# Moving the score stores of two batches from SyncE's DMA queue to ScalarE's, in a one-core talking-heads attention and expert kernel

## The chip, the cores and the metric

The kernel runs on one core of one Trainium2 chip. The metric is the device time of one execution in microseconds (us). Before the change three runs gave 1441.49 to 1446.57 us, with a median of 1444.0 us. The profile is of one further execution.

The engines are named as the profile names them: PE (TensorE; PEld is its weight load), DVE (VectorE), ACT (ScalarE), POOL (GpSimd) and SP (SyncE). SP computes nothing here: it issues DMAs. Before the change it issues every one of them.

## What is computed

```python
scores = np.matmul(q, k.transpose(0, 1, 3, 2)) / np.sqrt(64)   # q, k, v: 8 batches, 12 heads, 448, 64
scores = np.einsum('bhij,hg->bgij', scores, w_pre)             # mix the 12 heads
attn = np.exp(scores - np.max(scores, axis=-1, keepdims=True))
attn = attn / (np.sum(attn, axis=-1, keepdims=True) + 1e-09)
attn = np.einsum('bhij,hg->bgij', attn, w_post)                # mix them again
x = np.matmul(attn, v)                                         # heads side by side: 3584 x 768
h = (x @ w1) * (x @ w2) @ w3                                   # 768 -> 1024, 1024 -> 1024
out = h @ w_out                                                # 1024 -> 768
```

The weights w1, w2, w3 and w_out arrive as 64-bit numbers and are turned into 32-bit ones on the chip.

## The kernel before

**Scores.** `qk` (line 166) computes one score tile: two heads of a batch, the pair `p` (0 to 5), for 128 query rows, the tile `c`. Tiles 0, 1 and 2 are rows 0 to 383; `c == 3` joins the last 64 rows of two pairs. PE writes the two heads into two PSUM banks (`psq`), ACT copies them into an SBUF tile `st` (lines 179 and 180), and a DMA stores `st` in `raw_d[b]`, a DRAM array of all heads of a batch. `qk` doesn't issue this DMA: it returns a function, `store`, that does. The `st` tiles come from pools with two buffers: odd pairs of batch 0 have a pool of their own (`qp`), all others share `kp`. So the copy into a buffer waits until the store from it has landed.

**Rows read back.** The mixing works on 20 query rows of all 12 heads at a time, called a set. `fetch(m)` (line 195) reads the rows of set `m` from `raw_d` into `r`, of which there are two. `mix(m)` (line 214) multiplies them by w_pre into PSUM, `largest` and `exp` make the softmax, `scale` and `post` the second mixing, and `put` (line 272) copies the result into `mt`. `av` multiplies by v once 150 rows are there.

**Steps.** The loop at line 889 runs over steps `n`, two to a set. A step first does what is at its start: in an even step `fetch(m + 2)`, then `do_later()` (line 83), which calls the functions put aside, the stores of the step before among them, then loads of v and of the next q and k. Then come the pieces of weight conversion, softmax or second mixing, and background matmuls. Last come the `qk` of the step, whose `store` goes into `later` (line 982). So on SP a score store stands behind the fetch of the next step. Steps 0 to 11 have one `qk` of batch 0 each, steps 12 to 14 one for its last rows; batch 1 adds its own from step 11 on, about three in four steps.

**The first tile.** For `c == 0` of batch 0 all pairs go into one wide tile `sz`. Before the loop the upper 48 rows (`FIRST`) are stored pair by pair, and the other 80 rows of all heads by one DMA of 1680 KB, made at line 805 and issued where `held()` is called (line 881), after the fetches of sets 0 and 1 and one load of weight words.

**Weight words.** In the first steps `converting` (line 132) turns words into 32-bit weights: a load `cs`, up to five ahead, a square on ACT (`cm`, line 110), four operations on DVE (`cx`, lines 121 to 124) and a split into two parts by ACT (line 129) and POOL (line 130).

**DMA semaphores.** In the built program each DMA, on whichever queue, adds to one of eight semaphores, DMAHW0 to DMAHW7, mostly in turn, and first waits until the DMA before it on the same semaphore has landed. So a DMA waits, as a rule, for the one issued eight before it in the order of the program.

Of the kernel before, what the change touches and what calls it, by code (L numbers as in the profile page):

```python
# [21 lines left out]
QT, NJ = 128, 4  # L22
# [5 lines left out]
PP = 64  # L28
JB = S // PP
SETS = NB * B // 2  # L30
FIRST = 48
# [19 lines left out]
class Kernel:  # L51
# [114 lines left out]
    def qk(self, b, p, c, banks):  # L166


        nc = self.nc
        ps = [self.bank(i, f"psq{b}_{p}_{c}_{s}")[:, :S] for s, i in enumerate(banks)]  # L170
        for z, (t, q, k) in enumerate(self.parts(b, p, c)):
            for s in range(2):
                rows = slice(s * D, (s + 1) * D)
                nc.tensor.matmul(ps[s][z * PP:(z + 1) * PP], t[rows, q:q + PP], t[rows, k:k + S], start=True, stop=True)  # L174
        if b == c == 0:
            st = self.sz[:, 2 * p:2 * p + 2]
        else:
            st = (self.qp if b == 0 and p % 2 else self.kp).tile([128, 2, S], F32, tag="st", name=f"st{b}_{p}_{c}", bufs=2)
        nc.scalar.copy(st[:, 0], ps[0])  # L179
        (nc.vector.tensor_copy if b == c == 0 else nc.scalar.copy)(st[:, 1], ps[1])  # L180
        raw = self.raw_d[b]
        if c == 3:
            def store():
                for z in range(2):
                    nc.sync.dma_start(raw[3 * QT:, 2 * (p + z) - 2:2 * (p + z)], st[z * PP:(z + 1) * PP])
            return store
        n = QT if b or c else FIRST
        return lambda: nc.sync.dma_start(raw[c * QT:c * QT + n, 2 * p:2 * p + 2], st[:n])

# [549 lines left out]
    def run(self):  # L741
        nc, tc = self.nc, self.tc
# [52 lines left out]
        held = []  # L795
# [6 lines left out]
        next(fold_pieces)  # L802
        for f in held:
            f()
        held = lambda: nc.sync.dma_start(self.raw_d[0][FIRST:QT], self.sz[FIRST:])

# [3 lines left out]
        for b in range(1, B):  # L812
            first, per = (11, 28 / 21) if b == 1 else ((b - 1) * NB - 6, NB / 21)
            units = [(b, p, c) for g in range(0, HP, 2) for p, c in [*itertools.product((g, g + 1), range(3)), (g + 1, 3)]]
            for i, (b, p, c) in enumerate(units):
                n = int(first + i * per) | (b > 1)
# [3 lines left out]
        for b in range(B):  # L820
            for a in range(NG):
                for g in range(HP):
                    n = (b * NB + (a + 1) * GB + 3) | 1
# [54 lines left out]
            self.fetch(m)  # L878
        next(fold_pieces)
        next(fold_pieces)  # L880
        held()
        next(fold_pieces)
        next(fold_pieces)
        self.mix(0)
# [4 lines left out]
        for n in range(N + 6):  # L889
# [45 lines left out]
            p, pieces = self.n_made - 1 if fold_pieces else 2 * KF + 3 * KF, None  # L935
            if avs.get(n):
                pass
            elif fold_pieces:
                f = (self.n_made - 1 - 2 * KF) // 3
# [39 lines left out]
                self.mix(m + 1)  # L979
            self.do_ends()  # L980
            for i, x in enumerate(qks.get(n, [])):
                self.later.append(self.qk(*x, (6, 7) if i else (0, 1)))
            if third:
                next(unit_pieces)

# [66 lines left out]
```

## Time and profile before

| | |
|---|---|
| median of three runs | 1444.0 us |
| the three runs | 1446.57, 1441.49, 1444.0 us |
| profiled execution, its own time | 1437.83 us |
| its span, first to last instruction | 1436.1 us |
| PE busy | 1382.4 us, 96% |
| ACT busy | 832.4 us, 58% |
| DVE busy | 741.1 us, 52% |
| POOL busy | 620.3 us, 43% |
| granted PE clock, mean | 0.986 |

Times in the rows of the profile count from the start of the span. A timeline row gives start, duration, engine, line, operation, the tiles out and in, and in brackets how long the engine sat idle before it and what the profile takes to have ended that. "DMA share" in a table of windows is the mean busy share of the 16 DMA engines, "GB/s" what they moved, "(x...)" a number of instructions. "us to landing" counts from the issue of a DMA.

### The profile page before, as it was taken

Reading aid. Unit: us, or ns where it says so; the run is one execution under the profiler, and the core shown is the slowest. Engines: PE = TensorE matmul, PEld = TensorE weight load, DVE = VectorE, ACT = ScalarE, POOL = GpSimd, SP = SyncE. Lnnn points to the kernel's source line nnn. Section 1 sums busy time; section 2 is a strip of 40 time slices with the busy share of each in tenths; the row PEclk is TensorE's granted clock in tenths of the full one; section 3 lists DMA queues with packets and bytes.
Section 4 is the critical chain, followed back from the end, with each engine's and each line's share of the span. In section 5 each row is a group of like instructions: output and inputs, shape, how many; then the busy total and the mean of one; then the engine's idle time right before and its main releaser. Section 6 shows DMA issues by size and latency. Waiting matters only on the chain.

```text
span 1436.1 us, 45775 instructions
## 1 busy us (share of the span) xinstructions
PE 1382.4 (96%) x18684; PEld 1055.2 (73%) x18684; DVE 741.1 (52%) x1497; ACT 832.4 (58%) x1952; POOL 620.3 (43%) x754
## 2 busy tenths in 40 slices
PE   5889999999999999999999999999999999999998
PEld 2457786776677667776777777777777777899988
DVE  6867566767544544432444436334444446345563
ACT  4867666777766666665656556556555445422231
POOL 2433233434433544532345336334335446446693
PEclk7989999999999999999999999999999999999999
DMA  8998789999999999999989979799879757698775
GB/s 294 366 326 279 236 270 322 320 312 317 324 286 348 355 356 330 362 346 349 287 275 290 320 259 280 249 323 354 288 229 281 241 177 223 195 337 270 231 232 171
DMA packets 203761, 416.87 MB, mean 290 GB/s; under 512 B 20528, under 2 KB 120112, under 8 KB 203472
## 3 DMA queue, kind: packets, MB, share of 16 engines
q1 hardware_dynamic: 203552, 413.94, 87.6%
q8 instruction: 149, 2.44, 0.7%
q14 instruction: 60, 0.49, 0.1%
HBM read 279.77 MB, written 134.09 MB: 288 GB/s over the span
## 4 chain that ended last, share of the span: by engine, by line
PE 82%; DMA 8%; DVE 4%; ACT 2%; issue 1%; POOL 1%; SPq 0%; DVEq 0%; POOLq 0%; ACTq 0%
PE e L702 21%; PE psa L301 11%; PE pso L260 10%; PE psm L220 9%; PE psq L174 7%; PE eg L522 5%; PE psf L360 4%; PE eo L553 4%; PE e2o L702 4%; PE e1o L702 4%; PE e3o L702 4%; DMA wu<-w_d 3%; DMA r<-raw_d 2%; DMA raw_d<-st 2%; ACT e L235 1%
## 5 line engine op out<-in xcount | busy, mean ns | idle before, releaser
L247 POOL TENSOR_SCALAR w<-wpo,ri 128x60 f32<-128x60 f32 x360 | 180.7, 518 | 485.1 <-DVE ri L245 465.3
L227 DVE TENSOR_REDUCE mn<-psm 128x1 f32<-128x448 f32 x360 | 207.7, 618 | 321.6 <-PE psm L220 321.3
L274 ACT COPY mt<-pso 128x480 f32<-128x480 f32 x352 | 197.9, 621 | 185.8 <-PE pso L260 185.6
L702 PE MATMUL e<-eh,wu 128*128 128x448 f32 x1008 | 296.8, 371 | 6.4 <-DVE c L656 3.2
L235 ACT ACTIVATE e<-psm,mn 128x448 f32<-128x448 f32 x360 | 226.8, 643 | 7.9 <-DVE mn L227 7.9
L702 PEld LDWEIGHTS e<-eh,wu 128*128 128x128 f32 x1008 | 187.5, 188 | 52.2 <-issue 26.8
L260 PEld LDWEIGHTS pso<-w,e 60*64 60x64 f32 x10080 | 175.2, 135 | 51.0 <-issue 42.5
L220 PE MATMUL psm<-r,wsc 60*64 60x448 f32 (+1 forms) x1440 | 191.2, 550 | 19.1 <-DVE cx L124 8.3
L260 PE MATMUL pso<-w,e 60*64 60x60 f32 x10080 | 199.1, 224 | 0.4 <-ACT mt L274 0.3
L702 PE MATMUL e<-el,wu 128*128 128x448 f32 x504 | 186.9, 371 | 0.0
L301 PE MATMUL psa<-mt,v 128*64 128x150 f32 (+1 forms) x2304 | 156.9, 292 | 4.1 <-ACT st L179 4.1
L301 PEld LDWEIGHTS psa<-mt,v 128*64 128x64 f32 x2304 | 143.6, 137 | 20.1 <-ACT st L179 6.7
L174 PE MATMUL psq<-kq 64*64 64x448 f32 x1176 | 154.6, 542 | 2.4 <-ACT st L179 2.4
L656 DVE TENSOR_TENSOR c<-c,e 128x448 f32<-128x448 f32 x168 | 101.7, 618 | 87.7 <-PE e L702 82.9
L179 ACT COPY st<-psq 128x448 f32<-128x448 f32 x162 | 86.4, 533 | 73.7 <-ACT mt L274 34.1
L522 PE MATMUL eg<-xh,wu 128*128 128x448 f32 x384 | 119.2, 381 | 6.3 <-DMA wu<-w_d 6.3
L641 POOL TENSOR_TENSOR el<-x,eh 128x448 fp32r<-128x448 f32 x90 | 103.7, 1170 | 32.8 <-ACT eh L640 29.9
L702 PEld LDWEIGHTS e<-el,wu 128*128 128x128 f32 x504 | 94.6, 188 | 22.5 <-issue 14.1
L174 PEld LDWEIGHTS psq<-kq 64*64 64x64 f32 x1176 | 60.8, 135 | 56.4 <-issue 28.8
L522 PEld LDWEIGHTS eg<-xh,wu 128*128 128x128 f32 x384 | 71.9, 190 | 38.7 <-issue 24.0
L244 DVE TENSOR_SCALAR sa<-sm 128x2 f32<-128x2 f32 x180 | 34.9, 194 | 113.6 <-ACT e L235 113.1
L180 ACT COPY st<-psq 128x448 f32<-128x448 f32 x162 | 87.6, 541 | 0.0
(99 smaller groups left out, 2010.1 us busy)
## 6 DMA issues: line engine op xcount, KB each, us to landing
r<-raw_d SPq DMA_DIRECT2D x344, 210.0 KB, 5.1
raw_d<-st SPq DMA_DIRECT2D x138, 448.0 KB, 6.1
wu<-w_d SPq DMA_DIRECT2D x104, 384.0 KB, 6.7
wu<-s_d SPq DMA_DIRECT2D x96, 384.0 KB, 4.8
wu<-w_d SPq DMA_DIRECT2D x51, 512.0 KB, 5.5
kq<-kq SPq DMA_DIRECT2D x42, 448.0 KB, 7.0
wu<-s_d SPq DMA_DIRECT2D x36, 512.0 KB, 4.9
x<-x_d SPq DMA_DIRECT2D x72, 224.0 KB, 5.7
```

The costliest lines, as they stand in the source:

```text
L174: nc.tensor.matmul(ps[s][z * PP:(z + 1) * PP], t[rows, q:q + PP], t[rows, k:k + S], start=True, stop=True)
L220: nc.tensor.matmul(ps[s][c * PP:(c + 1) * PP, :S], self.wsc[k], r[k, c], start=True, stop=True)
L227: self.nc.vector.tensor_reduce(mn[:, s:s + 1], self.psm[m][s][:, :S], axis=AX.X, op=ALU.min)
L235: nc.scalar.activation(e, p[:, :S], AF.Exp, bias=mn[:, s:s + 1], scale=-1.0, accum_out=sm[:, s:s + 1])
L247: nc.gpsimd.tensor_scalar_mul(w2[:, s], self.wpo, ri[:, s:s + 1])
L260: nc.tensor.matmul(self.pso[c][z * PP:(z + 1) * PP, at:at + HK], e[k, j * PP:(j + 1) * PP], w2s[k, s], start=True, stop=True)
L274: self.nc.scalar.copy(dst.rearrange("p j g (s i) -> p j s g i", s=2), src)
L301: nc.tensor.matmul(self.psa[rows, g % 3, :W], v[:, j, rows], mt[:, j, 2 * g + s, :W], start=(j == 0), stop=(j == NJ - 1))
L522: nc.tensor.matmul(p, u[:, k % (K1 // 2), x], xs[y][:, k], start=(k == 0 and t == 0), stop=(k == K1 - 1 and t == 2))
L641: nc.gpsimd.tensor_tensor(lo, x, hi.bitcast(F32), op=ALU.subtract)
L656: nc.vector.tensor_tensor(a[out], a[to[0]], p, op=ALU.add)
L702: nc.tensor.matmul(p, w[:, k, x], ops[m, k][y], start=(k == 0 and t == 0), stop=(k == nk - 1 and t == 2))
```

## The change

Three edits move 44 DMA issues to ACT. First, the score stores of batches 0 and 1 are issued on ACT's DMA queue (`nc.scalar`), all but the upper 48 rows of the first tile. Second, in the loop these stores are called right behind the copies of their `qk`, and not put into `later`; those of batches 2 to 7 stay as they were. Third, the 80 lower rows of the first tile go out in two DMAs, of 16 and of 64 rows, also on ACT.

```diff
-        raw = self.raw_d[b]
-        if c == 3:
-            def store():
+        raw, dma = self.raw_d[b], nc.sync.dma_start if b > 1 or b == c == 0 else nc.scalar.dma_start
+
+        def store():
+            if c == 3:
                 for z in range(2):
-                    nc.sync.dma_start(raw[3 * QT:, 2 * (p + z) - 2:2 * (p + z)], st[z * PP:(z + 1) * PP])
-            return store
-        n = QT if b or c else FIRST
-        return lambda: nc.sync.dma_start(raw[c * QT:c * QT + n, 2 * p:2 * p + 2], st[:n])
+                    dma(raw[3 * QT:, 2 * (p + z) - 2:2 * (p + z)], st[z * PP:(z + 1) * PP])
+            else:
+                n = QT if b or c else FIRST
+                dma(raw[c * QT:c * QT + n, 2 * p:2 * p + 2], st[:n])
+
+        return store
...
-        held = lambda: nc.sync.dma_start(self.raw_d[0][FIRST:QT], self.sz[FIRST:])
+        held = [lambda k=k: nc.scalar.dma_start(self.raw_d[0][k], self.sz[k]) for k in (slice(FIRST, PP), slice(PP, QT))]
...
-        held()
+        for f in held:
+            f()
...
-                self.later.append(self.qk(*x, (6, 7) if i else (0, 1)))
+                store = self.qk(*x, (6, 7) if i else (0, 1))
+                if x[0] > 1:
+                    self.later.append(store)
+                else:
+                    store()
```

The new lines shift the code: line 188 of before is 189 of after, 202 is 205, 805 is 808.

The first place is SP's queue before the loop, before the change. `cs3` to `cs5` are loads of weight words, `r1` is the second set's rows, and L805 stores the 80 rows.

```order
L202 DMA r1_222<-raw0_d_62 60x2x448 [waits DMAHW6_49]
L103 DMA cs3_225<-wo 128x768
L805 DMA raw0_d_62<-sz_136 80x5376
L103 DMA cs4_238<-wo 128x768 [waits DMAHW1_49]
L103 DMA cs5_240<-wo 128x768 [waits DMAHW2_49,DVE_49,Activation_49]
```

After the change the 80 rows stand on ACT, as two DMAs between a square (`cm1`) and a split (`fw0`) of the weight conversion:

```order
L129 CAST fw0_227<-cx0_210 128x3x128 [waits DVE_49]
L110 ACTIVATE cm1_230<-cs1_151 128x384 [waits DMAHW1_49,Activation_49]
L808 DMA raw0_d_62<-sz_136 16x5376 [waits DMAHW5_49]
L808 DMA raw0_d_62<-sz_136 64x5376 [waits DMAHW7_49]
L129 CAST fw0_227<-cx1_232 128x3x128 [waits DVE_49]
L110 ACTIVATE cm2_245<-cs2_206 128x256 [waits DMAHW6_49,Activation_49]
```

On SP `cs4` now follows `cs3` directly.

The second place is SP at steps 10 to 13, before the change. In a name such as `st1_0_1` stand batch, pair and tile; `w34` is a stored piece of folded weights.

```order
L188 DMA raw0_d_62<-st0_4_2_784 128x896 [waits DMAHW1_49,Activation_49]
L286 DMA v0_5_789<-v 128x512 [waits DMAHW2_49]
L103 DMA cs18_791<-wo 128x768 [waits DMAHW3_49,DVE_49]
L202 DMA r8_863<-raw0_d_62 60x2x448 [waits DMAHW4_49,PE_49]
L202 DMA r8_863<-raw0_d_62 60x2x448 [waits DMAHW5_49]
L188 DMA raw0_d_62<-st0_5_2_851 128x896 [waits DMAHW6_49,Activation_49]
L188 DMA raw1_d_63<-st1_0_0_860 128x896 [waits DMAHW7_49,Activation_49]
```

After the change ACT has these stores, each behind its own two copies; here steps 10 and 11 on ACT:

```order
L179 COPY st0_4_2_785<-psq0_4_2_0_779 128x448 [waits PE_49]
L180 COPY st0_4_2_785<-psq0_4_2_1_780 128x448 [waits PE_49]
L189 DMA raw0_d_62<-st0_4_2_785 128x896 [waits DMAHW4_49,Activation_49]
L129 CAST fo_148<-cx13_769 128x384 [waits DVE_49]
L110 ACTIVATE cm14_803<-cs14_577 128x384
L277 COPY mt0_0_415<-pso0_141 128x4x2x12x5 [waits PE_49]
L277 COPY mt0_0_415<-pso1_142 128x4x2x12x5 [waits PE_49]
L179 COPY st0_5_2_852<-psq0_5_2_0_846 128x448 [waits DMAHW1_49,PE_49]
L180 COPY st0_5_2_852<-psq0_5_2_1_847 128x448 [waits PE_49]
L189 DMA raw0_d_62<-st0_5_2_852 128x896 [waits DMAHW0_49,Activation_49]
```

The store of `st0_5_2` no longer stands behind the fetch of `r8`; what ACT does next now stands behind the store and the semaphores that it waits for.

## The prediction

> **What bounds the kernel now.** I read the windows first, then the chain of waits of the first 110 us, then the timelines of ACT, SP and DVE around its longest pieces. The windows (engine busy times, granted clock, DMA share, GB/s):
>
> ```profile
> core 0: us, PE busy (x) PEld busy (x) DVE busy (x) ACT busy (x) POOL busy (x), PEclk, DMA share, GB/s
> 14.00:16.00 2.00, 0.00 (x0) 0.00 (x0) 1.86 (x4) 0.30 (x1) 0.58 (x1) 0.50 0.60 179
> 18.00:20.00 2.00, 1.84 (x9) 0.93 (x13) 0.09 (x1) 0.41 (x1) 0.72 (x1) 0.50 0.85 197
> 28.00:62.00 34.00, 29.02 (x424) 15.16 (x425) 31.95 (x63) 29.39 (x71) 14.25 (x19) 0.86 1.02 354
> 62.00:96.00 34.00, 25.42 (x294) 13.38 (x286) 23.54 (x44) 21.67 (x52) 11.53 (x14) 0.80 1.03 367
> 96.00:112.00 16.00, 15.06 (x263) 11.60 (x263) 7.27 (x15) 10.27 (x25) 3.77 (x6) 1.00 0.66 212
> 120.00:150.00 30.00, 30.00 (x403) 22.84 (x402) 24.17 (x48) 22.48 (x56) 10.84 (x15) 1.00 0.96 308
> 150.00:200.00 50.00, 49.36 (x686) 39.33 (x685) 30.66 (x64) 33.01 (x80) 14.44 (x21) 1.00 0.80 255
> ```
>
> Four stages follow. Until 28 us the DMA engines are not full and others wait. From 28 to 62 DVE is full (31.95 of 34), ACT nearly (29.39), and the DMA share is 1.02. From 62 to 96 PE, DVE and ACT all have idle time and only the DMA engines are full. From 96 PE is (15.06 of 16, 30.00 of 30). The stores moved are those of the first three stages and of the fourth up to about 190 us; what is won before 96 us should stay won, since PE then works through a fixed order.
>
> The chain of waits of that stretch (start, us, what):
>
> ```profile
> 17.18 0.42 SPq L805
> 17.65 10.36 DMA cs<-wo
> ...
> 60.76 8.07 DMA r<-raw_d
> 68.96 1.50 PE psm L220 x8
> 71.09 7.26 DMA raw_d<-st
> ...
> 87.56 8.09 DMA raw_d<-st
> 95.72 0.54 ACT st L179
> ```
>
> Its long pieces are transfers: a load of words issued behind the 80-row store, a fetch, and two score stores.
>
> **The change part by part.**
>
> *A, the first tile.* On DVE:
>
> ```profile
> 25.33 0.17 DVE L245 RECIPROCAL ri<-sa 128x2 f32<-128x2 f32 x1
> 28.10 0.36 DVE L121 TENSOR_SCALAR cx<-cs 128x384 int32<-128x384 int32 x1 [2.60 <-DMA cs<-wo]
> ```
>
> DVE waits 2.60 us for the load issued at 17.65. The 1680 KB ahead of it take 4.7 us at the 367 GB/s of 62 to 96. On ACT they stand behind the second square and so start some 2 to 3 us earlier, while the engines move only 179 and 197 GB/s, and the load no longer queues behind them. At best the 2.60 go. At worst half of the 4.7 us comes ahead of the fetches of the first sets and delays all by 2.3. Nearer the first, as the engines had room: **-1.5** (-2.6 to +2.3). The share below 1 between 14 and 20 us is also what limits it: no more than about 2 us of transfer time lay idle.
>
> *B, steps 0 to 10 (28 to 62 us).* The pace is that of DVE, and ACT waits twice in two steps:
>
> ```profile
> 36.93 1.14 DVE L227 TENSOR_REDUCE mn<-psm 128x1 f32<-128x448 f32 x2
> 43.69 1.14 DVE L227 TENSOR_REDUCE mn<-psm 128x1 f32<-128x448 f32 x2
> ...
> 40.73 0.51 ACT L129 CAST fo<-cx 128x384 fp32r<-128x384 f32 x1 [0.64 <-DVE cx L124]
> 43.80 0.51 ACT L129 CAST fo<-cx 128x384 fp32r<-128x384 f32 x1 [0.20 <-DVE cx L124]
> ```
>
> Two steps take 43.69 - 36.93 = 6.76 us; ACT's idle time in them is 0.64 + 0.20 = 0.84. The trace shows no DMA issued on ACT; the nearest rows are SP's issues of the same stores, with their times to landing (minimum, median, maximum):
>
> ```profile
> L188 SPq DMA_DIRECT2D raw_d<-st x23: 325/349/1124, 28.8 to 128.3; - x23
> L185 SPq DMA_DIRECT2D raw_d<-st x8: 451/452/673, 74.1 to 103.8; - x8
> DMA to landing us min/median/max: 2.9/6.3/8.1
> ```
>
> I take 0.35 to 0.45 us on ACT. A store also waits for the end of its copy, which the next instruction didn't (a copy of 0.55 us is followed after 0.42): 0.13 more. Two stores are 0.96 to 1.16 us against 0.84 idle, so 0.1 to 0.3 per two steps, 0.6 to 1.6 over five times two steps, if nothing hides it. The fetched scores stay ahead, and DVE feels ACT only late in its pair: **+0.5** (0 to +1.6). What ACT waits for on the semaphore of the eighth DMA back is the third rival.
>
> *C, steps 11 to 17 (62 to 96 us).* The groups of this stretch, with the idle time ahead of them, and the copies on ACT:
>
> ```profile
> L179 ACT COPY st<-psq 128x448 f32<-128x448 f32 x10 | 5.3, 535 | 12.3 <-DMA raw_d<-st 8.8 <-PE psm L220 2.9 <-PE psq L174 0.4
> L124 DVE SCALAR_TENSOR_TENSOR cx<-cm,cx 128x384 f32<-128x384 f32 x7 | 6.7, 952 | 8.5 <-ACT cm L110 7.9
> ```
>
> ```profile
> 59.82 0.57 ACT L180 COPY st<-psq 128x448 f32<-128x448 f32 x1
> 63.30 0.56 ACT L180 COPY st<-psq 128x448 f32<-128x448 f32 x1
> 70.45 0.53 ACT L179 COPY st<-psq 128x448 f32<-128x448 f32 x1 [2.90 <-PE psm L220]
> 74.11 0.53 ACT L179 COPY st<-psq 128x448 f32<-128x448 f32 x1 [2.69 <-DMA raw_d<-st]
> 78.42 0.53 ACT L179 COPY st<-psq 128x448 f32<-128x448 f32 x1 [1.48 <-DMA raw_d<-st]
> 86.13 0.54 ACT L180 COPY st<-psq 128x448 f32<-128x448 f32 x1
> 95.72 0.53 ACT L179 COPY st<-psq 128x448 f32<-128x448 f32 x1 [4.05 <-DMA raw_d<-st]
> ```
>
> and SP's issues of three of the stores:
>
> ```profile
> 62.38 0.34 SPq L188 DMA_DIRECT2D raw_d<-st  x1
> ...
> 66.84 0.33 SPq L188 DMA_DIRECT2D raw_d<-st  x1
> ...
> 71.09 1.30 SPq L188 DMA_DIRECT2D raw_d<-st  x2
> ```
>
> ACT's copies wait 12.3 us, nearly all for the store that still reads their buffer; DVE then waits for ACT's squares. The 2.90 at 70.45 I count as such too: a copy reads nothing of `psm`, and 62.38 plus a landing of 8.07 is 70.45. How late were the stores? Pair 4 of tile 2 was copied by 59.82 + 0.57 = 60.39 and stored at 66.84, 6.4 us later, since SP stood before the fetch at 60.76 and loads. Pair 5 was copied by 63.86 and stored at 71.09, 7.2 us later. The last was copied by 86.67 and stored at 87.56, only 0.9 later. Issued behind the copies, the stores free their buffers that much earlier: 2.90 + 2.69 + 1.48 go, with the remaining 8.8 - 2.69 - 1.48 - 4.05 = 0.6, and 0.9 of the last 4.05: 8.6 us, if nothing else is late.
>
> Next late are the DMA engines: their share was 1.03, and the bytes don't change. But the stores are what is waited for; the loads of words and of v that they now pass are wanted later, and from 96 to 112 the share is 0.66: 16 x 0.34 = 5.4 us of idle transfer time into which they can slide. The end without that is 0. I take **-4.5** (-8.6 to 0), inside the 5.4, since a DMA can lag by no more than eight behind.
>
> The Trainium skill, page "DMA: Bandwidth & Descriptors", section "Queues, rings and completion order", has each DMA engine alternate between the queues with work, packet by packet. Then a store alone on ACT's queue would not wait behind the loads on SP's, and more than 0.9 of the last 4.05 us would go; this trace has one queue and can't show it.
>
> *D, from 96 us.* Of the 44 issues some 19 are left, to about 190 us: 19 x (0.48 to 0.58) = 9 to 11 us on ACT, which idles 7.5 of 30 and 17 of 50 us there. PE waits for its copies in 100 to 200 us only here:
>
> ```profile
> PE psa L301 <- ACT st L179: 1.3, 2, 0.6
> ```
>
> If an issue slips in front of such a copy it adds about 0.5, at a few places: **+0.5** (0 to +2). SP's 43 issues fewer I cost at nothing: it waits, it isn't short of time.
>
> Sum: -1.5 + 0.5 - 4.5 + 0.5 = **-5.0 us**; the ends sum to -11.2 and +5.9. The profiled execution took 1437.83 us (span 1436.1), so it would take 1432.8. It lies 6.2 below the median of the three runs, and I carry the difference over: 1444.0 - 5.0 = **1439.0 us**. About 0.3%, 4.3 us, is what a measurement here can tell from no change.
>
> **The rivals.**
>
> *First: the transfers were full anyway.* For it: share 1.02 and 1.03 from 28 to 96 us, and a queue that never ran dry. Then stores landing earlier only make loads land later, which ACT and DVE wait for instead; C is 0, and the sum is -0.5: **1443.5**. Against it: what waits in C is stores, and 5.4 us of room follow.
>
> The Trainium skill, same page, section "Issuing engines are not separate DMA queues", says that DMAs from any engine run on the same 16 DMA engines and that spreading them saves only the usually small time of issuing. By it the move to ACT would be worth nothing, and this rival comes out; but the 6.4 and 7.2 us above are places in an order, not times of issuing.
>
> *Second: all of it.* C gives 8.6, A 2.6, and DVE's pace of 6.76 us holds through to step 18: about -10.5, **1433.5**. For it: DVE's idle time from 62 to 96 is 34 - 23.54 = 10.5. Against: 28 to 62 already needs a full DMA share at this pace.
>
> *Third: slower, ACT waits for DMAs.* A store on ACT waits until the DMA eight before it has landed, and ACT's next split, square and exponentials stand behind it, then DVE and PE; on SP only loads stood behind it. About eight DMAs are issued in two steps, so the one eight back had 6.76 us. Pieces of the chain landed after 7.26 to 10.36 us. There are 20 tiles to store between 28 and 96 us. With a mean landing of 7.6 us ACT waits 20 x 0.84 = 17 us, against the 12.3 that go: +4.5 in place of C's -4.5, sum +4, **1448**. It decides from a mean landing of 6.76 + 12.3/20 = 7.4 us on. For it: ACT has only 0.84 us to spare in two steps. Against: the median landing of these stores is 6.3, and SP, rid of them, issues its loads earlier.
>
> That the change doesn't do what it says is out: the rows of the order show the stores on ACT.
>
> **How the numbers follow.** Forecast 0.47 (its own range 1436 to 1442), first rival 0.26, second 0.15, third 0.12. Faster by over 0.3%: the second and three quarters of the forecast, 0.50; within: the first and the rest, 0.38; slower: 0.12. From 1433 to 1447 about 8 in 10 lie: it leaves out the better half of the second rival and most of the third, and takes in some 2 us of scatter (the runs lie within 2.6 of their median).
>
> **What would show it.** Right: in the profile after, ACT's copies wait for `raw_d<-st` some 3 us in all before 100 us; the wait for `cs<-wo` near 28 us shrinks; PE is full from about 91; DMA share 96 to 112 is higher. An issue on ACT takes 0.3 to 0.5 us. Wrong: ACT idles ahead of the stores or of what follows them, with loads as what ended it (third); the same idle time before other instructions (first).

## Result: slower by 0.7%, and the profile after

| | before | after |
|---|---|---|
| median | 1444.0 us | 1454.78 us |
| lowest and highest run | 1441.49 to 1446.57 | 1451.48 to 1457.25 |
| ratio, 95% interval | | 1.007, 1.0046 to 1.0094 |
| profiled execution | 1437.83 us | 1454.78 us |
| its span | 1436.1 us | 1453.0 us |

The forecast was 1439.0, with 1433 to 1447 around it; the time is above that range. The sign is that of the third rival.

The windows of the kernel after, with the columns as before:

```profile
core 0: us, PE busy (x) PEld busy (x) DVE busy (x) ACT busy (x) POOL busy (x), PEclk, DMA share, GB/s
28.00:62.00 34.00, 26.80 (x297) 12.27 (x290) 28.50 (x54) 24.52 (x60) 12.86 (x16) 0.85 1.00 337
62.00:96.00 34.00, 23.80 (x343) 12.20 (x345) 23.34 (x46) 24.79 (x59) 11.06 (x15) 0.90 1.00 345
96.00:112.00 16.00, 16.00 (x232) 13.09 (x225) 11.88 (x24) 10.69 (x26) 5.09 (x7) 0.92 0.78 241
120.00:150.00 30.00, 30.00 (x408) 22.84 (x400) 23.14 (x48) 22.30 (x54) 10.34 (x15) 1.00 0.95 307
```

The spans of the two traces differ by 16.9 us, the medians by 10.8: the traced execution of the kernel before took 6.2 us less than its median. What the edits did is read below from the first 150 us.

Count the matmuls, not the busy time: between 28 and 62 us PE now does 297, where it did 424. ACT does 60 instructions for 71 and is busy 24.52 us, 5 less. The stage that I had priced at half a microsecond is where work is lost. From 62 to 112 PE does 343 + 232 = 575 matmuls for 294 + 263 = 557, so 18 come back, and from 120 us on the two kernels go at one pace again.

The chain of waits of the kernel after, up to 68 us (start, us, what):

```profile
21.67 6.84 DMA cs<-wo
...
35.35 0.33 ACTq L189
35.72 0.52 ACT fo L129
...
50.47 6.78 DMA cs<-wo
...
61.35 6.40 DMA cs<-wo
67.83 0.33 ACTq L189
```

Before, the long pieces after 60 us were a fetch and two score stores of 7.26 and 8.09 us. The stores are gone from it. In their place stand loads of weight words, and issues on ACT, right ahead of the split (line 129) that waits behind them.

A convenient clock for all that follows is the start of the mixing of a set on PE (line 220 before, 223 after). For sets 0, 2, 6 and 10 of the kernel before:

```profile
18.16 1.85 PE L220 MATMUL psm<-r,wsc 60*64 60x448 f32 x5 [8.26 <-DVE cx L124]
34.31 0.95 PE L220 MATMUL psm<-r,wsc 60*64 60x448 f32 x8
60.29 1.77 PE L220 MATMUL psm<-r,wsc 60*64 60x448 f32 x8
100.38 0.54 PE L220 MATMUL psm<-r,wsc 60*64 60x448 f32 x1
```

and of the kernel after:

```profile
25.38 1.89 PE L223 MATMUL psm<-r,wsc 60*64 60x448 f32 x5 [15.58 <-DMA r<-raw_d]
40.22 1.77 PE L223 MATMUL psm<-r,wsc 60*64 60x448 f32 x8
69.82 1.22 PE L223 MATMUL psm<-r,wsc 60*64 60x448 f32 x5 [0.97 <-DMA r<-raw_d]
107.85 0.54 PE L223 MATMUL psm<-r,wsc 60*64 60x448 f32 x1
```

The delay is 7.2 us at set 0, 5.9 at set 2, 9.5 at set 6 and 7.5 at set 10. So the first tile's sets come 7.2 late (A), 3.6 more are lost in steps 4 to 12 (B), and 2.0 are won in the sets after that (C). These are delays and not yet prices: what part of one is caught up without the change, the runs below show. A delay at set 10 stays: PE is busy all the time from then on, and set 60, at 432.16 us before and 440.86 after, is 8.7 late.

The new issues on ACT (ns for one: minimum, median, maximum; then the first and the last start), the times to landing of the stores, and two stores in ACT's timeline:

```profile
L189 ACTq DMA_DIRECT2D raw_d<-st x30: 321/326/348, 31.7 to 182.0; - x30
...
DMA to landing us min/median/max: 3.4/5.4/7.5
```

```profile
47.38 0.56 ACT L180 COPY st<-psq 128x448 f32<-128x448 f32 x1
47.97 0.32 ACTq L189 DMA_DIRECT2D raw_d<-st  x1
48.33 0.52 ACT L129 CAST fo<-cx 128x384 fp32r<-128x384 f32 x1 [0.39 <-ACT st L180]
...
57.29 0.57 ACT L180 COPY st<-psq 128x448 f32<-128x448 f32 x1
59.46 0.33 ACTq L189 DMA_DIRECT2D raw_d<-st  x1
59.83 0.51 ACT L129 CAST fo<-cx 128x384 fp32r<-128x384 f32 x1 [1.97 <-DVE cx L123]
```

The first is a store without a wait: the split starts 0.95 us after the start of the copy, where an instruction followed after 0.42 before. So a store takes 0.53 us of ACT's order, as forecast. The second has a wait: the copy ends at 57.86 and the issue starts at 59.46, 1.6 us later. A timeline shows such a wait only as a gap ahead of the issue; the bracket on the next row names a releaser on DVE, but DVE's result is not what ACT stood for: the last operation on the tile that the split reads (line 124) ended at 57.31, and line 123 works on the next tile. Between the end of a copy and the issue behind it lie 3.7 us in all from 28 to 62 and 2.4 us from 62 to 112 (22 issues).

Two theories. Theory 1: the late start of set 0 is the loss. Theory 2: ACT's queue for the score stores is the loss, either by the time of its issues (2a) or because ACT stands ahead of them until the transfer eight back has landed (2b). Each kernel was timed beside the kernel before on the same chip; ratios are to that.

### The profile page after: what moved, and what is told of

It is laid out like the page before. It is cut to its first block, busy times and chain, and to the rows that moved or that the text cites. A ratio compares the mean times of both kernels' runs of the same rounds, so it can differ in the third digit from the quotient of the medians.

```text
span 1453.0 us, 45739 instructions
## 1 busy us (share of the span) xinstructions
PE 1386.7 (95%) x18684; PEld 1057.4 (73%) x18684; DVE 739.5 (51%) x1497; ACT 833.6 (57%) x1952; POOL 618.7 (43%) x754
## 4 chain that ended last, share of the span: by engine, by line
PE 78%; DMA 11%; DVE 4%; ACT 3%; issue 2%; SPq 1%; POOL 1%; ACTq 0%; DVEq 0%; POOLq 0%
PE e L705 20%; PE psa L304 10%; PE pso L263 10%; PE psm L223 8%; PE psq L174 7%; PE eg L525 5%; PE psf L363 4%; PE e1o L705 4%; PE e2o L705 4%; PE e3o L705 4%; PE eo L556 3%; DMA wu<-w_d 3%; DMA r<-raw_d 2%; DMA cs<-wo 2%; DMA raw_d<-st 1%
## 5 line engine op out<-in xcount | busy, mean ns | idle before, releaser
L223 PE MATMUL psm<-r,wsc 60*64 60x448 f32 (+1 forms) x1440 | 194.2, 555 | 27.7 <-DMA r<-raw_d 20.9
```

The source lines that it names most:

```text
L223: nc.tensor.matmul(ps[s][c * PP:(c + 1) * PP, :S], self.wsc[k], r[k, c], start=True, stop=True)
```

## Experiments

### The third edit alone, and all but the third

The first kernel is before with the third edit alone (the loop that issues the two is left out here):

```diff
-        held = lambda: nc.sync.dma_start(self.raw_d[0][FIRST:QT], self.sz[FIRST:])
+        held = [lambda k=k: nc.scalar.dma_start(self.raw_d[0][k], self.sz[k]) for k in (slice(FIRST, PP), slice(PP, QT))]
```

> The kernel before with the third edit alone: the 80 lower rows of the first tile on ACT's queue in two DMAs, every other store as before. Theory 1 (the first tile is the cause: its big transfer on a second queue starves the fetch of the first sets): the first mixing starts near 25.4 us, as in the changed kernel, not at 18.2; 5 to 9 us above before, about 1451. Theory 2 (the stores of the steps on ACT are the cause, ACT waits for the DMA eight back; the late first mixing is caught up later): within 2 us of before. Theory 3 (both about equally): 3 to 5 us above.

Measured: 1445.81 us, 1.0006 (0.9989 to 1.0022). Set 0 starts at 25.80 us, 7.6 late; set 6 at 64.54 is 4.3 late, set 10 at 101.23 only 0.9. The late start is there in full and, with the stores of the steps as before, nearly caught up. Theory 1 falls as the account of the whole loss. The 3.4 us won from set 6 to set 10 also show that a late kernel catches up there without the second edit.

The second is the kernel after with that edit undone, so the lower rows leave on SP as before:

```diff
-        held = [lambda k=k: nc.scalar.dma_start(self.raw_d[0][k], self.sz[k]) for k in (slice(FIRST, PP), slice(PP, QT))]
+        held = [lambda: nc.sync.dma_start(self.raw_d[0][FIRST:QT], self.sz[FIRST:])]
```

> The changed kernel with the third edit undone: the 80 rows go out on SP in one DMA as before; the stores of the steps stay on ACT. Theory 1: first mixing near 18.2 us; within 3 us of before, since the trace of the changed kernel loses 2.3 us between the mixings of sets 0 and 6 and wins 2.1 between those of sets 6 and 10. Theory 2: 6 to 11 us above before. Theory 3: 3 to 6 us above.

Measured: 1451.84 us, 1.0054 (1.0037 to 1.0071). Set 0 starts at 18.20 as before, but set 2 at 40.55 us, 6.2 late, set 6 12.4 late, and set 10 at 109.91, 9.5 late. The row of set 6:

```profile
72.73 1.64 PE L223 MATMUL psm<-r,wsc 60*64 60x448 f32 x5 [2.54 <-ACT e L238]
```

The chain of waits shows how set 2 comes late:

```profile
28.56 7.41 DMA cs<-wo
36.04 0.35 ACTq L189
36.43 0.52 ACT fo L129
...
37.02 1.01 POOL fo L130
...
38.08 1.01 PE psf L363 x2
39.08 1.74 PE pso L263 x56
40.83 1.50 PE psm L223 x8
```

ACT's copies for that store end at 31.6 us. The store's DMA has the same semaphore as a load of words that SP issued only at 28.56 and that lands at 36.0; ACT stands 4.43 us for it, a load whose conversion is the one after next. Behind the store stand the split, then POOL's part, then PE's background matmuls, and behind those, in PE's fixed order, the mixing of set 2. Two more such gaps follow at 60.6 (2.55 us) and 70.7 (2.43 us). From 28 to 112 us the gaps are 10.4 us and the issues 9.2. And the DMA engines have less to do (that the loads' buffers come free later is a reading, not shown):

```profile
28.00:62.00 34.00, 22.55 (x270) 10.51 (x268) 23.35 (x46) 20.28 (x48) 9.65 (x13) 0.84 0.95 318
```

The DMA share is 0.95 and 318 GB/s, for 1.02 and 354 before.

### The first tile otherwise

Two variants of the third edit alone: with the rows split by even and odd heads in place of rows (so that the pieces are one row of one head), and with its two DMAs two pieces of the conversion later in the program.

```diff
+        held = [lambda k=k: nc.scalar.dma_start(self.raw_d[0][FIRST:QT, k::2], self.sz[FIRST:, k::2]) for k in range(2)]
```

> As the third edit alone, the same 1680 KB at the same place on ACT, but split by even and odd heads and not by rows, so that each contiguous piece is 1.8 KB, as those of the fetch are, and not 21 KB. Theory 1a (queues take turns by packet, and the packets of the wide rows, 15 KB each in the trace, take nearly all turns from the 1.8 KB packets of the fetch): the first mixing starts near 20 to 22 us, 3 to 5 earlier than with wide rows, and the time is 1 to 5 us above before. Theory 1b (the bytes ahead or beside count, whatever their packets): near 25 us, 5 to 9 above before.

```diff
         next(fold_pieces)
         next(fold_pieces)
-        held()
         next(fold_pieces)
         next(fold_pieces)
+        for f in held:
+            f()
         self.mix(0)
```

> The third edit alone with the two DMAs two pieces of weight conversion later on ACT, behind the third square, so that the fetches of sets 0 and 1 are issued and about to land first. Theories 1a and 1b: the first mixing starts at 18 to 19 us; the load of words that waited 10.4 us behind the 80 rows lands 1 to 4 us earlier than in before; between 3 us below and 1 us above before. If a second queue harms by itself (issues on SP of over 1 us whatever the order): first mixing at 20 us or later, 2 us or more above before.

Measured: 1444.23 us, 0.9998 (0.998 to 1.0016), set 0 at 23.47 and set 10 at 97.83; and 1444.79 us, 1.0014 (0.9998 to 1.003), set 0 at 18.05 but set 1 at 31.44, set 10 at 104.88. The smaller pieces bring set 0 forward by 2.3 us, less than the 3 to 5 expected, and leave it 5.3 late; the place moves the delay from set 0 to set 1; and no time can be told from before.

### The place without ScalarE's queue

The stores right behind their copies, but on SP, the first tile as before:

```diff
-        raw, dma = self.raw_d[b], nc.sync.dma_start if b > 1 or b == c == 0 else nc.scalar.dma_start
+        raw, dma = self.raw_d[b], nc.sync.dma_start
```

> The second edit alone, all on SP: the stores of batches 0 and 1 are called right behind their copies, ahead of the next fetch, but issued on SP; the first tile as before. Theory 2 (ACT's waiting and issuing is what costs; the earlier place is worth something): SP waits in ACT's stead, the copies wait for stores 3 to 9 us less in all than in before, and the time is 1 to 5 us below before. Theory 4 (the earlier place is what costs: the fetch and the loads behind the stores come later): 4 us or more above before, like the kernel with the stores on ACT.

Measured: 1441.04 us, 0.9988 (0.9974 to 1.0003). Set 2 starts at 35.67, set 6 at 61.38, set 10 at 97.67, 2.7 before the kernel before.

```profile
28.00:62.00 34.00, 26.35 (x412) 13.69 (x414) 30.82 (x59) 28.36 (x68) 13.74 (x17) 0.94 1.02 353
```

PE's count between 28 and 62 us is 412, the DMA share 1.02. So the second edit by itself may win a little, though its interval reaches no change, and the queue loses it: 270 matmuls against 412 for one change of queue.

The whole kernel after with its score stores on SP (the same line of the diff), the lower rows still in two DMAs on ACT:

> The changed kernel with one thing undone: the stores of batches 0 and 1 are at their new place but on SP's queue; the first tile's lower rows still go out in two parts on ScalarE's queue. If ScalarE's queue for the 14 steps with stores is the whole loss, as the runs so far say, this gives back all of the 0.7%: the place -0.12%, the first tile +0.06%, so 0.9995 (0.9975 to 1.0015) against before. If the late start of the mixing adds to the loss only together with a ScalarE that is behind, the same; if it adds by itself in the presence of the new place, 1.002 and more.

Measured: 1445.43 us, 1.0009 (0.9992 to 1.0027); set 0 at 26.68, set 10 at 101.16. The 0.7% is given back, but for an amount inside the interval. ACT's queue for the score stores is the loss. The late start is not free beside the new place: against the kernel with the first tile as before (set 10 at 97.67, 0.9988) set 10 is 3.5 us later, PE does 375 matmuls between 28 and 62 us for 412, and the ratio is 0.0021 higher, with intervals that just overlap.

### What of the queue: the time of the issues

First, before with one copy of 448 columns more on ACT behind each tile of batches 0 and 1 (two for `c == 3`), and no DMA on ACT; then the same copies in the kernel with the stores at the new place on SP:

```diff
+        if b == 1 or b == 0 and c:
+            for z in range(2 if c == 3 else 1):
+                nc.scalar.copy(st[:, 0], st[:, 0])
```

> The kernel before, all stores on SP, with one more copy on ACT (a half of the score tile onto itself, 448 columns, some 0.5 us) behind the two copies of each tile of batches 0 and 1, two behind those of the joined last rows: it takes ACT's time as an issue does (0.55 us in the trace of the changed kernel), but waits for no DMA. Theory 2a (the time of the issues on ACT is the cost): 5 to 9 us above before. Theory 2b (the waits for the DMA eight back, 10 us in the trace of the kernel with the first tile as before, are the cost): 0 to 3 us above before.

> The stores stand at their new place but on SP's queue, and ScalarE gets one copy of 448 columns more behind each tile of batches 0 and 1 (two behind c == 3), in place of the issue; it never waits for a DMA ahead of a store. Theory 1 (the loss of the changed kernel has two parts that add up, the time of the issues in ScalarE's order and its waits for the transfer eight back): the place gives -0.12%, the extra copies +0.34% as in their own run, so 1.002 (1.0005 to 1.0035) against before, clearly below the 1.0054 of the kernel with the stores on ScalarE's queue and the first tile as before. Theory 2 (what costs is only ScalarE's extra time, and the waits for the transfers are idle time that it would have had anyway): the same as with the real issues, 1.0045 to 1.006. Theory 3 (the place gives more as soon as ScalarE falls behind, since the copies then no longer wait for their buffers): 0.999 to 1.0005.

Measured: 1447.08 us, 1.0034 (1.002 to 1.0048), set 10 at 101.93; and 1443.56 us, 0.9996 (0.9976 to 1.0017), set 10 at 99.51. The first by itself spoke for 2a: with the stores at the old place ACT's extra time costs some 5 us. The second doesn't: with them at the new place 0.0008 of 1443 us, about 1 us, is left, less than the interval. That is below the 1.002 of theory 1 of that text, whose range the interval still reaches, and far from its theory 2 (1.0045 to 1.006). At the new place ACT's own time is not the loss, or only a small part of it: the same copies in place of the issues leave PE 406 matmuls between 28 and 62 us. Why they cost more at the old place is open; of the first kernel's 5 us its trace has only 1.6 at set 10.

### Other queues and other places

The same stores at the new place on POOL's queue, where in the built program they wait for the copies alone and for none of the eight semaphores:

```diff
-        raw, dma = self.raw_d[b], nc.sync.dma_start
+        raw, dma = self.raw_d[b], nc.sync.dma_start if b > 1 or b == c == 0 else nc.gpsimd.dma_start
```

> The same stores at the same place, right behind their copies, on POOL's queue: in the built program these wait for the copies alone and not for one of the eight semaphores. Theory 2b: ACT's idle time ahead of its splits goes; between 4 us below and 1 us above before. Theory 2a: the same, since ACT issues nothing. Theory 4: 4 us or more above before. POOL's own issue may cost 1 us and delay the splits behind it: then DVE and PE wait for POOL, and it says nothing.

Measured: 1445.31 us, 1.0016 (0.9999 to 1.0034); set 10 at 100.94, PE's count from 28 to 62 us 408. A queue of their own for the stores does not by itself lose those matmuls.

Next, only the stores of batch 1 and of batch 0's last rows on ACT, all else as before; none of them comes before 62 us:

```diff
+        act = b == 1 or b == 0 and c == 3
-        raw = self.raw_d[b]
+        raw, dma = self.raw_d[b], nc.scalar.dma_start if act else nc.sync.dma_start
...
-                self.later.append(self.qk(*x, (6, 7) if i else (0, 1)))
+                store = self.qk(*x, (6, 7) if i else (0, 1))
+                if not (x[0] == 1 or x[0] == 0 and x[2] == 3):
+                    self.later.append(store)
+                else:
+                    store()
```

> Only the stores of batch 1 and of the joined last rows of batch 0 go out on ACT right behind their copies (from step 11 on); tiles 1 and 2 of batch 0 and the first tile as before. Theory 2 with what the trace of the changed kernel shows (2 us lost before the mixing of set 6, 2 won behind it): 1 to 4 us below before. If the stores on ACT cost wherever they stand: 2 us or more above before.

Measured: 1447.28 us, 1.0037 (1.0024 to 1.005); the expected gain did not come. Set 6 starts at 60.63, set 7 at 76.27 (68.96 before), set 10 at 105.68. One row of SP's timeline, and ACT's around the first of these stores:

```profile
66.46 0.38 SPq L372 DMA_DIRECT2D w_d<-fz  x1
```

```profile
66.02 0.54 ACT L180 COPY st<-psq 128x448 f32<-128x448 f32 x1
74.25 0.36 ACTq L190 DMA_DIRECT2D raw_d<-st  x1
74.64 0.51 ACT L129 CAST fo<-cx 128x384 fp32r<-128x384 f32 x1 [8.09 <-DMA w_d<-fz]
```

The store is ready at 66.56. The transfer eight back in the program, a store of folded weights on SP, was issued at 66.46: SP was late itself. ACT stands 7.69 us, until it lands. Behind ACT's split and square stand the exponentials of set 6, whose PSUM banks PE needs for set 7:

```profile
76.27 2.38 PE L224 MATMUL psm<-r,wsc 60*64 60x448 f32 x8 [7.83 <-ACT e L239]
```

### Making the eighth transfer back nearer

The second kernel above (stores on ACT, first tile as before) with a load of 128 x 8 elements on SP ahead of each store of the loop, and the same loads with the stores on SP:

```diff
+                    junk = self.kp.tile([128, 8], F32, tag="junk", name=f"junk{n}_{i}", bufs=8)
+                    nc.sync.dma_start(junk, self.wpost[:, :8])
                     store()
```

> The kernel with the stores on ScalarE's queue and the first tile as before (1.0054), with one load of 128 x 8 elements more on SP just ahead of each store of batches 0 and 1: it moves 4 KB, but it takes one of the eight places in the round of transfers, so that the transfer eight back from a store was issued later and has less time to land. Theory 1 (ScalarE's waits for the transfer eight back cost some 4 us of the loss): the waits ahead of the stores between 28 and 112 us grow from 10 us to 15 us and more, and the kernel takes 3 to 10 us more, 1.0075 to 1.012. Theory 2 (those waits cost nothing): 1.004 to 1.0065, as without the extra loads, whatever the waits.

> The same extra loads of 128 x 8 elements, with all the stores at their new place on SP's queue, so that only SP waits for the transfer eight back. Theory 1 (it is ScalarE's waiting that costs, not that of SP): within 0.2% of the kernel with the stores on SP at the new place (0.9988), so 0.998 to 1.001. Rival (the extra loads themselves cost, in SP's order or at the DMA engines): 1.002 to 1.006, and the kernel with the extra loads and ScalarE's queue can then not be read against ScalarE's waits.

Measured: 1458.35 us, 1.0099 (1.0069 to 1.0129), gaps of 13.5 us between 28 and 112 us (10.4 without the loads, 15 and more expected); and 1447.71 us, 1.0019 (1.0001 to 1.0038). The pair differs by 0.8%, which is what the queue costs here. But the loads by themselves added 0.0045 with ACT's queue and 0.0031 without it: by their own effect on the waits this pair decides nothing.

### Waits without a queue

The stores on SP at the new place, and ACT reads one column of a word tile behind each tile's copies: of the tile for the conversion after next, or of the next one (`self.asked[0]`).

```diff
+                    if len(self.asked) > 1:
+                        junk = self.kp.tile([128, 1], F32, tag="junk", name=f"junk{n}_{i}", bufs=2)
+                        nc.scalar.copy(junk, self.asked[1][:, :1, 0].bitcast(F32))
```

> All stores at the new place but on SP's queue (0.9988), and ScalarE issues no DMA; behind the copies of each tile of batches 0 and 1 it reads one column of the word tile that is to be converted the time after next, so that it stands until that load has landed, as the store of the second tile stood at 36.0 us for a load issued at 28.6. Theory 1 (what costs is that ScalarE stands for a load that it does not yet need, with the conversion that PE needs behind it): the start of mixing of set 2 falls from 35.7 to 38 us or later, PE does 350 matmuls or fewer between 28 and 62 us (412 without the read), and the time is 1.002 to 1.006. Theory 2 (the queue itself costs, by its large packets or by SP's waiting in turn for ScalarE's stores): no loss beyond the 0.2 us of the read, 0.998 to 1.001, and set 2 within 1 us of 35.7.

> The same reads of one column, but of the word tile that ScalarE squares next anyway: the read adds its 0.2 us and no wait that would not come a moment later. Both theories: 0.998 to 1.001, set 2 within 1 us of 35.7 us, 390 or more matmuls on PE between 28 and 62 us. If this one is as slow as the other, the read's own time or the word tile's buffer coming free later is what costs, and the pair tells nothing of the wait.

Measured: 1445.16 us, 1.0015 (1.0 to 1.003), set 2 at 37.27, set 10 at 98.64, 356 matmuls from 28 to 62; and 1443.77 us, 1.0004 (0.9986 to 1.0021), set 2 at 36.23, 412 matmuls. The first read of the one, and of the other:

```profile
29.75 0.19 ACT L992 COPY junk<-cs 128x1 f32<-128x1 f32 x1 [4.66 <-DMA cs<-wo]
```

```profile
28.85 0.19 ACT L992 COPY junk<-cs 128x1 f32<-128x1 f32 x1 [3.10 <-DMA cs<-wo]
```

Of the 4.66 us only 0.9 is new: ACT would have stood for the next word tile anyway. The reads put 8.6 us of waiting on ACT, the control 3.1; set 2 came 1 us later than in the control, between what the two theories needed. The kernel did not make the long wait that it was built for.

### One store alone

All stores on SP at the new place, but one alone on ACT. The first two should wait, the third should not:

```diff
-        raw, dma = self.raw_d[b], nc.sync.dma_start
+        raw, dma = self.raw_d[b], nc.scalar.dma_start if (b, p, c) == (1, 0, 0) else nc.sync.dma_start
```

> All the stores at their new place on SP's queue (0.9988), except one alone on ScalarE's queue: that of tile c = 0 of pair 0 of batch 1, the one ahead of which ScalarE stood 7.7 us in the kernel with only the late stores on its queue. The transfer eight back from it is SP's store of pair 4 of the tile before. Theory 1 (ScalarE waits there for a transfer eight back that SP, itself late, has only just issued, and the exponentials and the mixing of set 7 stand behind it): a wait of 4 us or more ahead of that one store, set 7 at 73 us or later (69.96 with it on SP), set 10 later by 2 us or more, and 1.001 to 1.004 against before. Theory 2 (one issue costs its 0.35 us, and only the number of issues or the queue's whole traffic matters): 0.9975 to 1.0005, set 7 within 1 us of 69.96.

> The same, with the store of the second tile of c = 1 (pair 1 of batch 0) alone on ScalarE's queue, ahead of which ScalarE waited 4.43 us, to 36.0 us, with all on its queue. Theory 1 (the wait comes from the order of the transfers and not from the traffic on ScalarE's queue): a wait of 3 us or more, set 2 at 38 us or later (35.7 with it on SP); the time 0.999 to 1.003, since 50 us are left to catch up before set 10. Theory 2 (no wait for one store): set 2 within 1 us of 35.7, 0.9975 to 1.0005.

> The same, with one other store alone on ScalarE's queue: that of the first tile of c = 1 (pair 0 of batch 0), ahead of which ScalarE waited 0.03 us in the kernel with all 14 steps' stores on its queue. Both theories: no wait, 0.9975 to 1.0005, set 2 within 1 us of 35.7 us. It is the control of the single store that should wait.

Around the store of pair 0 of batch 1 (ACT's timeline):

```profile
65.62 0.60 ACT L180 COPY st<-psq 128x448 f32<-128x448 f32 x1
73.14 0.35 ACTq L189 DMA_DIRECT2D raw_d<-st  x1
73.53 0.51 ACT L129 CAST fo<-cx 128x384 fp32r<-128x384 f32 x1 [7.31 <-DMA raw_d<-st]
```

and around that of pair 1 of batch 0:

```profile
30.41 0.54 ACT L180 COPY st<-psq 128x448 f32<-128x448 f32 x1
35.48 0.34 ACTq L189 DMA_DIRECT2D raw_d<-st  x1
35.86 0.51 ACT L129 CAST fo<-cx 128x384 fp32r<-128x384 f32 x1 [4.91 <-DMA raw_d<-st]
```

| store on ACT | gap | set that is late | set 10 | ratio, interval |
|---|---|---|---|---|
| none | | | 97.67 us | 0.9988 (0.9974 to 1.0003) |
| batch 0, pair 0, c = 1 | 0.03 us | none | 97.35 | 0.9988 (0.9973 to 1.0003) |
| batch 0, pair 1, c = 1 | 4.53 us | set 2, 39.99 for 35.67 | 100.84 | 1.0005 (0.9993 to 1.0018) |
| batch 1, pair 0, c = 0 | 6.92 us | set 7, 75.15 for 69.96 | 100.00 | 1.0000 (0.9985 to 1.0015) |

The rows of these sets, set 2 and set 7 first with all stores on SP, then set 2 with pair 1 of batch 0 and set 7 with pair 0 of batch 1 alone on ACT:

```profile
35.67 0.97 PE L223 MATMUL psm<-r,wsc 60*64 60x448 f32 x8
69.96 2.24 PE L223 MATMUL psm<-r,wsc 60*64 60x448 f32 x8 [2.08 <-DMA r<-raw_d]
...
39.99 1.77 PE L223 MATMUL psm<-r,wsc 60*64 60x448 f32 x8
...
75.15 2.38 PE L223 MATMUL psm<-r,wsc 60*64 60x448 f32 x8 [7.04 <-DMA raw_d<-st]
```

The last bracket names a store that landed at 75.12. But set 6's first exponential, behind ACT's split, ends with its sum at 75.09 here and at 76.22 in the kernel with the late stores, and PE starts 0.06 and 0.05 us later: it is the likelier releaser.

A single issue with 0.35 us on ACT costs nothing that can be told; a single issue with a wait delays its set by 4.3 or 5.2 us, of which 3.2 and 2.3 are left at set 10. In the time this is not clear: the intervals overlap, and 1.0000 lies below the 1.001 to 1.004 that theory 1 expected for the late store. One store makes the wait, so neither the traffic on ACT's queue nor the number of issues is needed for it: the order of the transfers is enough. The transfer need not be the same. Pair 1's store stood for a load of words when all stores were on ACT; alone there, by the profile, for SP's store of the tile before, issued at 29.00 and landed at 35.41. At set 2 this one wait makes most of the delay: 4.3 us, where all stores on ACT make 4.9 (40.55 for 35.67).

### What the runs add up to

The delay at set 10 against the kernel before goes roughly with the time; no kernel is off by more than 3.9 us. Eight kernels, and the three others that fit worst:

| kernel | set 10, us | its delay | ratio less 1, in us of 1443 |
|---|---|---|---|
| stores on ACT, extra loads | 112.70 | +12.3 | +14.3 |
| stores on ACT, first tile as before | 109.91 | +9.5 | +7.8 |
| the changed kernel | 107.85 | +7.5 | +10.1 |
| late stores on ACT | 105.68 | +5.3 | +5.3 |
| extra loads, stores on SP | 102.63 | +2.3 | +2.7 |
| stores on SP, lower rows on ACT | 101.16 | +0.8 | +1.3 |
| lower rows on ACT alone | 101.23 | +0.9 | +0.9 |
| stores on SP at the new place | 97.67 | -2.7 | -1.7 |
| copies more on ACT, stores at the old place | 101.93 | +1.6 | +4.9 |
| reads of the word tile after next | 98.64 | -1.7 | +2.2 |
| lower rows on ACT, later | 104.88 | +4.5 | +2.0 |

Each delay is of one execution. The kernel with the stores on SP at the new place, 2.7 us ahead of before at set 10 and 2.3 at set 66, is 4.4 behind at the last set, though its median is not above that of before. Every trace here drifts so behind the one of before after set 66, by 1 to 13 us, and 7.6 us of drift are in the third edit alone, where no store of the steps moved. So most of the loss is made before set 10, and made by ACT's queue. That ACT stands for transfers it doesn't need, and that this delays the mixing, is shown by the two single stores. How much of the 0.66% between the kernels with the stores on SP and on ACT these waits make is not settled: the two single waits came to 0.17% and 0.12%. What is left falls to the other gaps, to the 9.2 us of issues on an ACT that is already behind, and to loads that may then fall behind too; these were not told apart.

## Why the prediction was wrong

**What bounds the kernel** held: the four stages are there, and a delay at the end of the third stays.

**A (-1.5, -2.6 to +2.3)** failed in the trace; what it cost in time is small and not settled. Set 0 came 7.2 us late, three times the upper end. The working let at most half of the 80 rows' 4.7 us come ahead of the fetches. Both DMAs left ahead of the first fetch, at 13.01 and 14.42 us, and SP's issues of the four fetches, before and after, were:

```profile
14.95 1.74 SPq L202 DMA_DIRECT2D r<-raw_d  x4
...
14.94 6.68 SPq L205 DMA_DIRECT2D r<-raw_d  x4
```

The next load of words on SP, issued at 16.73 us before, left at 21.67 and landed at 28.5, and ACT stood 10.18 us for it; the load that was to gain, which had landed at 28.0, stands behind that one. The working also did not look at how the queues share. Between 12 and 30 us of the kernel after the two queues (packets, MB, share) are:

```profile
q1 hardware_dynamic: 1797, 3.20, 54.6%
q10 hardware_dynamic: 112, 1.72, 42.3%
```

A packet on ACT's queue is on average 1.72 MB / 112 = 15.4 KB, one of SP's 1.8 KB. The Trainium skill, page "DMA: Bandwidth & Descriptors", section "Queues, rings and completion order", says that a DMA engine alternates packet by packet; by that, as an estimate from these two sizes, a fetch gets about a tenth (1.8 of 17.2 KB) of an engine that both use, if what the trace counts as a packet is what the engine alternates by, which no run here shows. The variant with small pieces agrees in direction: set 0 came 2.3 us sooner; the other 5.3 are not explained. By the third edit alone 0.9 us of the delay are left at set 10; beside the new place on SP it made 3.5.

**B (+0.5, 0 to +1.6)** is the step that failed. Its own price of a store, 0.5 us of ACT, was right (0.33 us for the issue, 0.53 in ACT's order). What it put at nothing and left to the third rival, ACT's wait for the eighth transfer back, came here and not in the average way that the rival took. In the kernel after 3.6 us were lost from set 2 to set 6. With the first tile as before, set 2 alone is 6.2 us late, behind one gap of 4.43 us, and set 6 12.4 late, where B allowed 1.6.

**C (-4.5, -8.6 to 0)** is not shown to have come. ACT's copies between 62 and 96 us, and DVE's step behind the squares:

```profile
L179 ACT COPY st<-psq 128x448 f32<-128x448 f32 x11 | 5.9, 533 | 4.4 <-DMA cs<-wo 1.6 <-PE psq L174 1.6 <-issue 1.2
L124 DVE SCALAR_TENSOR_TENSOR cx<-cm,cx 128x384 f32<-128x384 f32 x7 | 7.0, 1006 | 9.3 <-ACT cm L110 9.3
```

The 8.8 us for `raw_d<-st` are gone and the idle time ahead of them fell from 12.3 to 4.4 (on SP, at the same place, 8.1 us of waits for `raw_d<-st` stay). The stores issued from 60 to 100 us also landed sooner, after 4.5 us at the median for 6.9 before. But DVE still waits 9.3 us for ACT's squares, 7.9 before; that ACT's time went into its issues and their waits is the likely reason. The 2.0 us won from set 6 to set 10 don't show C, since the third edit alone won 3.4 there with the stores as before. The place alone, on SP, which does not move set 0, gave 2.7 us at set 10 and 1.7 us (0.12%) of time, whose interval reaches no change.

**D (+0.5)** was near: from set 10 to set 11 the delay grows by 0.8 us, to 8.2 (110.54 and 118.77), it is 8.7 at set 60, and PE's counts from 120 to 150 us are 403 and 408.

**The first rival** (1443.5) is not excluded for the place alone (1441.04, interval up to 1.0003). The Trainium skill, page "DMA: Bandwidth & Descriptors", section "Issuing engines are not separate DMA queues", treats the time of issuing as the small thing that moves with the engine. The trace agrees on it, with 0.33 us; what the trace shows beside it is that the wait ahead of the issue moves too, here from SP onto ACT.

**The third rival** named the mechanism and got 0.12. I weighed it by a mean: 6.76 us since the eighth transfer back, a median landing of 6.3, so no wait. Three things in that failed. The transfer eight back in the program is not eight back in time: SP issued it 0.1 us before the store was ready in one case, 3 us before in another. The rule "from a mean landing of 7.4 us" did not have to be met: the landings behind two of the long waits are 7.41 us and some 7.8, within the 8.1 of the stores before. And the price of a wait is not its length shared over 20 stores but what stands behind the one that waits: a split, a square, two exponentials, and through them PE's next set. Few waits, not one at every store: 6.1 us of gaps in all in the kernel after, where the rival had 17. The rival's sum, +4, was short as well: +10.8 was measured.

## To carry to other kernels

When a DMA moves to another engine's queue, its semaphore wait moves with it: find the transfer that it waits for, when that is issued (a late queue issues late), and what on the new engine stands behind the wait. Here SP, which only issues, could stand, and ACT, which feeds DVE and PE, could not, though the issue itself takes 0.33 us. To win the place in the order, try the place first and keep the queue; and read a gain or a loss off a point from which the pace is fixed (set 10 here), not off where the first delay shows.

## What I had not expected of the hardware

- Stores that leave in rows of all heads went out in packets of 15.4 KB on ACT's queue, beside 1.8 KB for the fetches; set 0's mixing then came 7.2 us later. Single issues of the fetches on SP beside them took up to 2.50 us, for 0.37 to 0.42 before; with small pieces the four took 6.95 us, no less, so the size of the packets is not what stretches them.

- A start that is 7.6 us late at 18 us was worth 0.9 us at 100 us, while a delay of 6.2 us at 34 us grew to 9.5. In the first ACT goes on without the stores' waits; that this is what decides was not tested by itself.
- Extra time on ACT cost 0.34% with the stores at the old place, and nothing measurable at the new one.
